# Token lists compacted by a one-hot product and stored as 16 runs, and queries scaled ahead, in a retention + experts + bilinear kernel

## The chip, the cores and the metric

One core of a Trainium2 chip runs the whole kernel. Its engines work from queues of their own: TensorE (PE) multiplies matrices into PSUM banks, VectorE (DVE) and ScalarE (ACT) do elementwise work, GpSimd (POOL) does elementwise work and issues indirect DMAs, and SyncE (SP) issues most of the other DMAs. The metric is device microseconds of one launch, the median of three runs.

## The reference

Three parts follow each other. `q`, `k`, `v` are 4 x 8 x 768 x 64.

```
# retention, per batch and head; gamma[h] = 1 - 2**(-5-h)
state = gamma*state + outer(k[t], v[t]);  y[t] = (q[t] @ state)/sqrt(64)
# x: 3072 tokens x 512. Top-1 of 8 experts, 512 -> 1024 -> 512
logits = x @ w_gate + bias[modality];  e = argmax(logits)
g = 1/(sum(exp(logits - max)) + 1e-9)
out[mask_e] = g * (relu(x[mask_e] @ w1[e]) @ w2[e])
# bilinear layer on the 3072 rows
y = ((x @ m1) * (x @ m2)) @ w3 @ w_out
```

## The kernel before

**Attention.** The 3072 tokens are 24 tiles of 128, six for each batch. A tile's decay is split: `vprime` multiplies the values by gamma^-(position) on POOL, and the result of a tile is multiplied by a table `gtab[t % 6]` that holds gamma^(position)/8. The loop over `t` from -1 to 24 issues, in a fixed order that no scheduler changes, work of several tiles: `scores(t+1)` (k transposed by q, masked on VectorE into `at`), `rows_gate(t-1)`, `attend_T(t)` (state by q), `attend_v(t)` (masked scores by v', then `xT` on VectorE with the table), and `state(t+1)`. `rows_gate` multiplies `xT` by the identity and the gate's columns at once: ScalarE copies the rows `xr` out and issues their store to `x_scratch`, VectorE sums the logits into `L`. The transposed keys `kT` of every tile are loaded beside `qkv`.

**Fold.** w3 @ w_out is computed on the chip. The weights come as float64 bits: `f64_f32` decodes a piece in three VectorE passes, ScalarE casts the high part, and the low part is a subtraction (POOL in the loop, VectorE after it). Seven of the twelve pieces are decoded between the tiles; `fold_mm(n)` then issues n of 64 units of three products, the counts being the list `FM`.

**Token lists.** Tiles are routed in batches of 8, 7, 6 and 3. `route_a` finds the expert of each token as a one-hot row `OH`, and running counts `RS`; `route_b` turns them into the place of each token in its expert's list. `scatter_ids(t)` stores 128 pairs (token, gate), 8 bytes each, to their places in `tok_scratch`, one indirect DMA a tile; the 24 are declared free of each other. After the loop `tables1` computes which list piece each slot takes and gathers the pieces (`lists`), `tables2a` and `tables2b` make the control rows `ctl`, `tables3` the gather indices, and the expert slots begin, whose products fill TensorE up to the end. `cld` keeps the lists in slot order, and is read back near the end for the final scatter.

Order around the change: the loop body and the calls behind it, as the program's text has them; each engine takes its instructions in that order. Rotating PSUM banks (`bank()`, five) and tile pools of fixed depth (`QB` for qkv, three `xr`) make later instructions wait for earlier readers.

Of the kernel before, what the change touches and what calls it, by code (L numbers as in the profile page):

```python
# [18 lines left out]
P = 128  # L19
B, H, S, D = 4, 8, 768, 64  # L20
NT = B * S
E = 8
# [13 lines left out]
LOAD_T = [2, 5, 8, 10, 13, 15, 18, 20, 22]  # L36
SPLIT_T = [5, 8, 10, 13, 15, 18, 20]
QB, KB, FB = 7, 5, 5
# [14 lines left out]
for _n, _w in (("ident", 128), ("sl", 128), ("ones", 128), ("desc", 8), ("er", 8), ("kp", NPAIR), ("le", 64), ("gt", 64), ("p", 1), ("tok", NTILE)):  # L53
    CB[_n] = (_o, _o + _w)
    _o += _w
# [3 lines left out]
def const_tables():  # L59
# [27 lines left out]
    put(b, CB, "er", (e * R)[None, :])  # L87
# [4 lines left out]
    put(b, CB, "p", i[:, None])  # L92
    return a.astype(np.float32), b.astype(np.float32)


def pack(q, k, v, moe_modality_id, moe_w_gate, moe_modality_bias, moe_w1, moe_w2, moe2_w1, moe2_w2, moe2_w3, moe2_w_out):
# [7 lines left out]
    kT = qt(k)  # L104
# [7 lines left out]
    def bits(a):  # L112
# [9 lines left out]
        "mod": moe_modality_id.reshape(NTILE, P).T,  # L122
        "mbias": moe_modality_bias.reshape(1, 16),
        "wg": kmaj(moe_w_gate, 4),
    }
FM = [6, 12, 8, 8, 8, 6]


def kernel(tc, a, out):
# [3 lines left out]
    with ExitStack() as ctx:  # L133
# [39 lines left out]
        RS = ct([P, NTILE + 1, E], F32, "RS")  # L173
# [3 lines left out]
        dsti = ct([P, NTILE], I32, "dsti")  # L177
        tg = ct([P, NTILE, 2], F32, "tg")
        cg = ct([P, NTILE, 2], F32, "cg")
# [3 lines left out]
        lists = fold.tile([P, T2, 2], F32, name="lists")  # L183
# [11 lines left out]
        def f64_f32(pool, tag, s, nm, done, bufs=2):  # L195
            d = pool.tile([P, 1024], U32, tag=tag, name="dec" + nm, bufs=bufs)
            V.tensor_scalar(d, s[:, :, 1], 3, 0x3FFFFFFF, op0=ALU.logical_shift_left, op1=ALU.bitwise_and)
            yield
            V.scalar_tensor_tensor(d, s[:, :, 1], 0xC0000000, d, op0=ALU.bitwise_and, op1=ALU.bitwise_or)
            yield  # L200
            V.scalar_tensor_tensor(d, s[:, :, 0], 29, d, op0=ALU.logical_shift_right, op1=ALU.bitwise_or)
            yield from done(d.bitcast(F32))
# [84 lines left out]
        none = lists[:TR + 1]  # L287
        st = {}

        def load(t):  # L290
            s = st.setdefault(t, {})
            s["kT"] = pa.tile([P, 4, P], F32, tag="kT", name=f"kT{t}", bufs=KB)
            nc.sync.dma_start(s["kT"].rearrange("p a i -> p (a i)"), a["kT"][t])
# [32 lines left out]
        def attend_v(t):  # L326
# [7 lines left out]
            V.tensor_tensor(s["xT"], b, gtab[t % NC], op=ALU.mult)  # L334
# [18 lines left out]
        def rows_gate(t):  # L353
            s = st[t]
            xr = pa.tile([P, 4, P], F32, tag="xr", name=f"xr{t}", bufs=3)
# [7 lines left out]
            nc.scalar.dma_start(xd[t * P:t * P + P, :], xr.rearrange("p a w -> p (a w)"))  # L363
# [3 lines left out]
        def route_a(t0, t1):  # L367
            sl, sh = slice(t0, t1), [P, t1 - t0, E]
            V.tensor_tensor(L[:, sl], L[:, sl], biasm[:, sl], op=ALU.add)
            V.tensor_reduce(mx[:, sl, 0], L[:, sl], axis=AX.X, op=ALU.max)  # L370
            V.tensor_tensor(tmp[0][:, sl], L[:, sl], bc(mx[:, sl], sh), op=ALU.is_equal)
            V.tensor_tensor(tmp[0][:, sl], tmp[0][:, sl], bc(CV("desc").unsqueeze(1), sh), op=ALU.mult)
            V.tensor_reduce(dst[:, sl, 0], tmp[0][:, sl], axis=AX.X, op=ALU.max)
            V.tensor_tensor(OH[:, sl], tmp[0][:, sl], bc(dst[:, sl], sh), op=ALU.is_equal)
            for t in range(t0, t1):
                V.tensor_tensor(RS[:, t + 1, :], RS[:, t, :], OH[:, t, :], op=ALU.add)
            V.tensor_tensor(tmp[1][:, sl], L[:, sl], bc(mx[:, sl], sh), op=ALU.subtract)
            nc.scalar.activation(tmp[1][:, sl], tmp[1][:, sl], AF.Exp)

        def route_b(t0, t1):  # L380
            sl, sh, w = slice(t0, t1), [P, t1 - t0, E], (t1 - t0) * E
            b = bank()
            nc.tensor.matmul(b[:, :w], lhsT=CV("sl"), rhs=OH[:, sl].rearrange("p t e -> p (t e)"), start=True, stop=False)
            nc.tensor.matmul(b[:, :w], lhsT=CV("ones"), rhs=RS[:, sl].rearrange("p t e -> p (t e)"), start=False, stop=True)
            V.tensor_reduce(dst[:, sl, 0], tmp[1][:, sl], axis=AX.X, op=ALU.add)
            V.tensor_scalar(dst[:, sl, 0], dst[:, sl, 0], 1e-9, None, op0=ALU.add)
            V.reciprocal(tg[:, sl, 1], dst[:, sl, 0])
            V.tensor_tensor(tmp[0][:, sl], b[:, :w].rearrange("p (t e) -> p t e", e=E), bc(CV("er").unsqueeze(1), sh), op=ALU.add)
            V.tensor_tensor(tmp[0][:, sl], tmp[0][:, sl], OH[:, sl], op=ALU.mult)
            V.tensor_reduce(dst[:, sl, 0], tmp[0][:, sl], axis=AX.X, op=ALU.add)  # L390
            V.tensor_copy(dsti[:, sl], dst[:, sl, 0])
# [5 lines left out]
        def scatter_ids(t):  # L397
            nc.gpsimd.memset(pad, 0.0)
# [816 lines left out]
```

## Time and profile before

| | us |
|---|---|
| median of 3 runs (884.88 to 885.59) | 885.41 |
| the profiled execution | 886.3 |
| its span | 884.2 |
| TensorE busy / VectorE / ScalarE / GpSimd | 839.0 / 478.6 / 286.8 / 342.0 |

The span runs from the first to the last recorded instruction. Busy time of TensorE is modelled at its ends; a gap between two of its instructions is a wait. "Releaser" is what ended the idle time ahead of an instruction, inferred from semaphores. DMA share is the mean busy share of the 16 DMA engines.

### The profile page before, as it was taken

Reading aid. Unit: us, or ns where it says so; the run is one execution under the profiler, and the core shown is the slowest. Engines: PE = TensorE matmul, PEld = TensorE weight load, DVE = VectorE, ACT = ScalarE, POOL = GpSimd, SP = SyncE. Lnnn points to the kernel's source line nnn. Section 1 sums busy time; section 2 is a strip of 40 time slices with the busy share of each in tenths; the row PEclk is TensorE's granted clock in tenths of the full one; section 3 lists DMA queues with packets and bytes.
Section 4 is the critical chain, followed back from the end, with each engine's and each line's share of the span. In section 5 each row is a group of like instructions: output and inputs, shape, how many; then the busy total and the mean of one; then the engine's idle time right before and its main releaser. Section 6 shows DMA issues by size and latency. Waiting matters only on the chain. (4 is left out here: it accounts for less than half of the span.)

```text
span 884.2 us, 16215 instructions
## 1 busy us (share of the span) xinstructions
PE 839.0 (95%) x6240; PEld 767.5 (87%) x6240; DVE 478.6 (54%) x697; ACT 286.8 (32%) x514; POOL 342.0 (39%) x324
## 2 busy tenths in 40 slices
PE   5988788899999999999999999999999999999997
PEld 5988687689999999899999977887887888999996
DVE  4476586764432516751111653255237375999993
ACT  1232232143213222722211533142223343455541
POOL 4238184223005041814100314246326354666563
PEclk9999899999999999999999999999999999999999
DMA  8999984778236445754326029714111514744411
GB/s 304 323 409 235 322 210 99 204 271 310 89 121 215 144 160 198 268 190 154 111 61 252 26 62 408 277 55 155 60 58 50 156 48 143 236 159 155 144 51 58
DMA packets 63187, 153.67 MB, mean 174 GB/s; under 512 B 10675, under 2 KB 22963, under 8 KB 61544
## 3 DMA queue, kind: packets, MB, share of 16 engines
q1 hardware_dynamic: 51736, 122.64, 41.1%
q0 software_dynamic: 7888, 23.36, 7.7%
q10 hardware_dynamic: 3456, 6.29, 2.3%
q8 instruction: 60, 0.98, 0.5%
q14 instruction: 47, 0.39, 0.1%
HBM read 102.73 MB, written 49.58 MB: 172 GB/s over the span
## 5 line engine op out<-in xcount | busy, mean ns | idle before, releaser
L235 PE MATMUL b<-h,wh 128*128 128x256 f32 x768 | 139.8, 284 | 1.4 <-PE b L645 0.7
L851 PE MATMUL al<-xh,ws 128*128 128x512 f32 x384 | 125.1, 394 | 2.0 <-DMA ws<-ws_scratch 1.4
L235 PEld LDWEIGHTS b<-h,wh 128*128 128x128 f32 x768 | 119.8, 192 | 2.2 <-ACT h L760 0.9
L761 DVE SCALAR_TENSOR_TENSOR h<-b,h 128x512 fp32r<-128x512 f32 x48 | 32.6, 688 | 158.1 <-ACT h L760 155.9
L235 PE MATMUL b<-xh,wl 128*128 128x256 f32 x384 | 108.8, 283 | 0.3 <-DVE wl L206 0.3
L235 PE MATMUL b<-xh,wh 128*128 128x256 f32 x384 | 108.8, 283 | 0.1
L235 PE MATMUL b<-h,wl 128*128 128x256 f32 x384 | 108.7, 283 | 0.1
L235 PE MATMUL b<-xl,wh 128*128 128x256 f32 x384 | 108.7, 283 | 0.0
L851 PEld LDWEIGHTS al<-xh,ws 128*128 128x128 f32 x384 | 72.2, 188 | 19.3 <-issue 1.8
L851 PE MATMUL al<-xl,ws 128*128 128x512 f32 x192 | 75.6, 394 | 0.0
L1135 PE MATMUL oa<-wfh,ab 128*128 128x256 f32 x384 | 74.9, 284 | 0.7 <-DVE ot L1142 0.6
L235 PEld LDWEIGHTS b<-xh,wl 128*128 128x128 f32 x384 | 73.7, 192 | 0.5 <-DVE wl L206 0.5
L235 PEld LDWEIGHTS b<-xh,wh 128*128 128x128 f32 x384 | 73.6, 192 | 0.4 <-issue 0.3
L235 PEld LDWEIGHTS b<-xl,wh 128*128 128x128 f32 x384 | 73.6, 192 | 0.0
L235 PEld LDWEIGHTS b<-h,wl 128*128 128x128 f32 x384 | 73.7, 192 | 0.0
L851 PE MATMUL ga<-xh,ws 128*128 128x512 f32 x192 | 63.7, 392 | 2.3 <-ACT p L964 1.7
L1135 PEld LDWEIGHTS oa<-wfh,ab 128*128 128x128 f32 x384 | 61.6, 189 | 2.6 <-DVE ot L1142 2.0
L760 ACT ACTIVATE h<-b 128x512 fp32r<-128x512 f32 x48 | 28.4, 596 | 86.4 <-PE b L235 84.8
L206 POOL TENSOR_TENSOR wo<-dec,wo 128x512 fp32r<-128x512 f32 x12 | 16.6, 1393 | 99.5 <-ACT wo L205 99.5
L1135 PE MATMUL oa<-wfl,ab 128*128 128x256 f32 x192 | 54.0, 281 | 0.0
L796 ACT COPY yT<-b 128x512 f32<-128x512 f32 x24 | 14.1, 588 | 118.7 <-PE b L235 106.0
L636 POOL DMA_INDIRECT xg<-x_scratch,gidx x28 | 28.0, 1001 | 63.1 <-PE b L645 44.2
(224 smaller groups left out, 1887.2 us busy)
## 6 DMA issues: line engine op xcount, KB each, us to landing
qkv<-in_qkv SPq DMA_DIRECT2D x22, 768.0 KB
ws_scratch<-wo SPq DMA_DIRECT2D x28, 512.0 KB
ws<-ws_scratch SPq DMA_DIRECT2D x28, 512.0 KB
raw<-in_wall SPq DMA_DIRECT2D x24, 512.0 KB
ab<-ab_scratch SPq DMA_DIRECT2D x24, 512.0 KB
f64f<-in_w SPq DMA_DIRECT2D x8, 1024.0 KB
f64m<-in_m SPq DMA_DIRECT2D x16, 512.0 KB
y_scratch<-yT SPq DMA_DIRECT2D x14, 512.0 KB
```

Of the source, the lines that this page charges most:

```text
L206: lo_eng.tensor_tensor(lo, src, hi.bitcast(F32), op=ALU.subtract)
L235: nc.tensor.matmul(b, lhsT=x, rhs=y, start=first and n == 0, stop=last and n == 3 * len(ks) - 1)
L636: nc.gpsimd.indirect_dma_start(out=xgs[j][y], out_offset=None, in_=xd, in_offset=bass.IndirectOffsetOnAxis(ap=gidx[:, y, j:j + 1], axis=0))
L760: nc.scalar.activation(h, b, AF.Relu)
L761: V.scalar_tensor_tensor(l, b, 0.0, h.bitcast(F32), op0=ALU.max, op1=ALU.subtract)
L796: nc.scalar.copy(yT[:, 2 * dp:2 * dp + 2, :].rearrange("p a t -> p (a t)"), b)
L851: nc.tensor.matmul(b, lhsT=y, rhs=r[:, kk, :], start=first and n == 0, stop=n == 5, skip_group_check=True)
L1135: nc.tensor.matmul(b, lhsT=x[:, k], rhs=y[:, k], start=first and n == 0, stop=n == 11, skip_group_check=True)
```

## The change

1. **Lists.** The rank of a token is now counted inside a group of 1, 2 or 3 tiles (`GROUPS`). `places` compares the ranks with a row of numbers, which gives a one-hot matrix 128 x w for each tile; `entries` multiplies `OHV` (expert one-hot times token number, and times gate: 16 columns) by it, so that 16 rows, two for each expert, hold that group's entries in order and densely. They are copied to `ls` and stored with one indirect DMA as 16 runs of w numbers, each at its offset `gix`; a later run writes over the unused end of an earlier one, so the stores are in turn. Token and gate lists lie apart, in two halves of `tok_scratch`, and `tables1` gathers twice.
2. **Queries.** `decayed` multiplies q in place by the table ahead of the scores, on VectorE, two or three tiles early; `xT` becomes a ScalarE copy.
3. **Work dealt out.** Route operations, one-hot rows and decoding are generators with a cost each; `spend` takes up to 2.4 us of them a tile.
4. **Others.** Keys 0 to 3 are transposed on TensorE instead of loaded; constants are loaded in parts; the x stores go from ScalarE's queue to SP's; the low part of the weights goes to VectorE; six buffers for qkv, four for kT, two for xr; `FM` changes; the lists are read back as 24 rows and transposed.

```diff
-LOAD_T = [2, 5, 8, 10, 13, 15, 18, 20, 22]
-SPLIT_T = [5, 8, 10, 13, 15, 18, 20]
-QB, KB, FB = 7, 5, 5
+LOAD_T = [0, 1]
+SPLIT_T = [2, 4, 6, 8, 10, 13, 16]
+BUDGET = 2.4
+QB, KB, FB = 6, 4, 5
+GROUPS = [(1,) * 8, (2, 2, 3), (3, 3), (3,)]
-FM = [6, 12, 8, 8, 8, 6]
+FM = [3, 22, 12, 8, 8, 6]
...
+        def decayed(t, eng=V):
+            q = st[t]["qT"]
+            eng.tensor_tensor(q, q, gtab[t % NC], op=ALU.mult)
...
-            V.tensor_tensor(s["xT"], b, gtab[t % NC], op=ALU.mult)
+            if t:
+                nc.scalar.copy(s["xT"], b)
+            else:
+                V.tensor_tensor(s["xT"], b, gtab[0], op=ALU.mult)
...
-            nc.scalar.dma_start(xd[t * P:t * P + P, :], xr.rearrange("p a w -> p (a w)"))
+            nc.sync.dma_start(xd[t * P:t * P + P, :], xr.rearrange("p a w -> p (a w)"))
...
+        def places(g0, g1):
+            w, ohs = (g1 - g0) * P, []
+            for t in range(g0, g1):
+                oh = pa.tile([P, 3 * P], F32, tag="oh", name=f"oh{t}", bufs=3)[:, :w]
+                V.tensor_scalar(oh, io[:, :w], rk[:, t], None, op0=ALU.is_equal)
+                ohs.append(oh)
+            return ohs
+
+        def entries(x, g0, g1, ohs):
+            w = (g1 - g0) * P
+            b = bank()[:2 * E, :w]
+            for i, oh in enumerate(ohs):
+                nc.tensor.matmul(b, lhsT=OHV[:, g0 + i].rearrange("p z e -> p (z e)"), rhs=oh, start=i == 0, stop=i == g1 - g0 - 1)
+            ls = pa.tile([2 * E, 3 * P], F32, tag="ls", name=f"ls{g0}", bufs=1)[:, :w]
+            nc.scalar.copy(ls, b)
+            nc.gpsimd.indirect_dma_start(out=tbl.rearrange("r i -> (r i)").rearrange("(r w) -> r w", w=w), out_offset=bass.IndirectOffsetOnAxis(ap=gix[:, x:x + 1], axis=1), in_=ls, in_offset=None)
...
-        def scatter_ids(t):
-            nc.gpsimd.memset(pad, 0.0)
-            i = nc.gpsimd.indirect_dma_start(out=tblf, out_offset=bass.IndirectOffsetOnAxis(ap=dsti[:, t:t + 1], axis=0), in_=tg[:, t, :], in_offset=None)
-            no_dep(i.ins, "ids", "each scatter writes entries of its own")
...
+        def decoded(x):
+            g = fold_split(x, V)
+            yield from timed(g, (.7, 1.2, 1.2))
+            late.append(g)
+            more.append(x + 2)
...
+            if t >= 1:
+                spend(BUDGET)
...
         t0, t1 = bounds[-2], bounds[-1]
-        route_a(t0, t1)
+        run(routed(t0, t1))
+        for r in ready:
+            route_exp(*r)
         fold_mm(FM[0])
-        route_b(t0, t1)
-        for t in range(t0, t1):
-            scatter_ids(t)
+        b = route_mm(t0, t1)
+        ready.clear()
+        run(settled(t0, t1, b))
+        routes_done()
         tables1()
```

VectorE in the middle of the loop, about one turn and a half, before (`at` is the mask, `L` the gate reduce, `decf` a decoded piece):

```order
L315 TENSOR_TENSOR at_1022<-b_1023,ca_sb 128x4x128
L315 TENSOR_TENSOR at_1022<-b_1024,ca_sb 128x4x128
L362 TENSOR_REDUCE L<-r_1037 128x8
L334 TENSOR_TENSOR xT_1059<-b_1046,g_97 128x512
L315 TENSOR_TENSOR at_1077<-b_1078,ca_sb 128x4x128
L315 TENSOR_TENSOR at_1077<-b_1079,ca_sb 128x4x128
L197 TENSOR_SCALAR decf_1092<-f64f_1012 128x1024
L362 TENSOR_REDUCE L<-r_1095 128x8
L334 TENSOR_TENSOR xT_1117<-b_1104,g_98 128x512
L199 SCALAR_TENSOR_TENSOR decf_1092<-f64f_1012,decf_1092 128x1024
```

The same place after the change (`oh` is a one-hot row block, `wol` the low part of a weight piece):

```order
L343 TENSOR_TENSOR at_950<-b_951,ca_sb 128x4x128
L343 TENSOR_TENSOR at_950<-b_952,ca_sb 128x4x128
L393 TENSOR_REDUCE L<-r_964 128x8
L322 TENSOR_TENSOR qkv_817<-qkv_817,g_97 128x512
L467 TENSOR_SCALAR oh_1000<-io_sb,rk 128x128
L226 TENSOR_TENSOR wol_93<-decf_815,woh_89 128x1024
L201 TENSOR_SCALAR decf_1005<-f64f_686 128x1024
L203 SCALAR_TENSOR_TENSOR decf_1005<-f64f_686,decf_1005 128x1024
L343 TENSOR_TENSOR at_1014<-b_1015,ca_sb 128x4x128
L343 TENSOR_TENSOR at_1014<-b_1016,ca_sb 128x4x128
```

The xT multiply out of a bank is gone; a multiply of qkv in SBUF, the one-hot rows and the low part have come in between the gate reduce and the next mask.

ScalarE in the loop, two turns before (`xr` are the rows, `T` the state):

```order
L361 COPY xr_1036<-r_1037 128x256 x2
L363 DMA x_scratch<-xr_1036 128x512
L351 COPY T_102<-acc_886 64x4x64 x2
L361 COPY xr_1094<-r_1095 128x256 x2
L363 DMA x_scratch<-xr_1094 128x512
L351 COPY T_101<-acc_886 64x4x64 x2
```

And after (`ls` is the list of one group):

```order
L392 COPY xr_1027<-r_1028 128x256 x2
L477 COPY ls_1039<-b_1037 16x128
L363 COPY xT_1055<-b_1042 128x512
L382 COPY T_100<-acc_926 64x4x64 x2
L224 CAST w3h_1003<-decf_1005 128x1024
L392 COPY xr_1093<-r_1094 128x256 x2
L477 COPY ls_1105<-b_1103 16x128
L363 COPY xT_1121<-b_1108 128x512
L382 COPY T_101<-acc_926 64x4x64 x2
```

The list copy and the xT copy stand between the rows and the state copies, and the store of the rows is no longer in this queue.

TensorE behind the loop, around the last batch's rank products, before (the fold's products are those of `woh`, `wol`):

```order
L246 MATMUL b_1611<-wol_93,w3h_1090 128x512
L246 MATMUL b_1611<-woh_89,w3l_1091 128x512
L383 MATMUL b_1630<-OH,cb_sb 128x24
L384 MATMUL b_1630<-RS,cb_sb 128x24
L417 MATMUL b_1646<-RS,cb_sb 128x8
L246 MATMUL b_1611<-woh_90,w3h_1090 128x512
L246 MATMUL b_1611<-wol_94,w3h_1090 128x512
```

And after:

```order
L251 MATMUL b_1758<-wol_91,w3h_1003 128x512
L251 MATMUL b_1758<-woh_87,w3l_1004 128x512
L435 MATMUL b_1768<-OH,cb_sb 128x24
L437 MATMUL b_1768<-rel,cb_sb 128x24
L439 MATMUL b_1768<-cb_sb,RS 16x1
L475 MATMUL b_1786<-oh_1780,OHV 16x384
L475 MATMUL b_1786<-oh_1782,OHV 16x384
L475 MATMUL b_1786<-oh_1784,OHV 16x384
L498 MATMUL b_1793<-RS,cb_sb 128x8
L251 MATMUL b_1758<-woh_87,w3h_1003 128x512
```

The three list products of the last group stand between its rank products and the totals (L417, now L498), and so ahead of most of the fold; six more of them stand ahead of the first fold product.

## Rows read from the trace of the kernel before

**Rows 1.** Windows: busy us and instructions by engine, granted clock, DMA share, GB/s

```profile
0.00:26.09 26.09, 16.19 (x168) 15.05 (x168) 9.95 (x17) 3.58 (x8) 10.52 (x17) 0.87 0.86 298
26.09:145.10 119.01, 103.56 (x1304) 94.53 (x1300) 81.33 (x170) 35.38 (x90) 56.89 (x61) 0.96 0.93 285
145.10:199.40 54.30, 49.02 (x231) 40.46 (x230) 37.15 (x78) 14.28 (x21) 15.88 (x22) 0.97 0.64 202
199.40:884.20 684.80, 670.20 (x4546) 617.51 (x4544) 350.17 (x433) 233.60 (x395) 258.75 (x225) 1.00 0.42 148
28.00:64.00 36.00, 34.62 (x474) 31.86 (x472) 23.22 (x48) 10.22 (x28) 9.61 (x8) 1.00 0.98 375
72.00:96.00 24.00, 19.15 (x256) 17.35 (x254) 14.28 (x22) 6.77 (x16) 15.70 (x19) 0.95 1.06 202
```

**Rows 2.** Timeline of TensorE, one tile: start, us, engine, line, operation, tiles

```profile
30.69 1.16 PE L313 MATMUL b<-qkv,kT 64*128 64x128 f32 x16
31.78 1.19 PE L359 MATMUL r<-iwg,xT 128*128 128x136 f32 x8
32.81 1.05 PE L324 MATMUL b<-qkv,T 128*128 128x128 f32 x8
33.80 1.09 PE L332 MATMUL b<-at,vp 128*64 128x128 f32 x16
34.72 0.63 PE L348 MATMUL acc<-vp,qkv 128*64 128x64 f32 x16
35.29 0.94 PE L313 MATMUL b<-qkv,kT 64*128 64x128 f32 x12
```

**Rows 3.** The token list's DMAs: ns min/median/max, first and last start; landing

```profile
L399 POOL DMA_INDIRECT tok_scratch<-tg,dsti x24: 954/999/1829, 69.0 to 155.9; - x24
...
DMA to landing us min/median/max: 5.4/11.8/12.7
```

**Rows 4.** Timeline of POOL, the first v' product

```profile
9.21 1.04 POOL L304 TENSOR_TENSOR vp<-qkv,ca_sb 128x512 f32<-128x512 f32 x1 [7.37 <-DMA qkv<-in_qkv]
```

**Rows 5.** Timeline, 15 to 19 us: POOL's decay tables beside VectorE's bias work

```profile
15.11 3.15 POOL L506 TENSOR_TENSOR g<-ca_sb 128x512 f32<-128x512 f32 x3
...
15.22 1.15 DVE L539 TENSOR_TENSOR biasm<-mf,mb_sb 128x192 f32<-128x192 f32 x1
...
18.51 0.36 DVE L542 TENSOR_TENSOR biasm<-biasm,tmp 128x192 f32<-128x192 f32 x1
```

**Rows 6.** Timeline of VectorE in that tile; then one group of its lines

```profile
30.40 0.69 DVE L334 TENSOR_TENSOR xT<-b,g 128x512 f32<-128x512 f32 x1 [1.11 <-PE b L332]
...
31.89 1.29 DVE L315 TENSOR_TENSOR at<-b,ca_sb 128x512 f32<-128x512 f32 x2 [0.79 <-PE b L313]
...
33.69 0.19 DVE L362 TENSOR_REDUCE L<-r 128x8 f32<-128x32 f32 x1 [0.52 <-ACT xr L361]
...
L201 DVE SCALAR_TENSOR_TENSOR decf<-f64f,decf 128x1024 uint32<-128x1024 uint32 x7 | 8.6, 1223 | 0.2
```

**Rows 7.** Landing of plain stores and loads of another scratch tensor

```profile
DMA to landing us min/median/max: 2.6/3.5/5.0
```

**Rows 8.** Timeline of TensorE: control rows, and one unit of the fold

```profile
164.54 0.45 PE L457 MATMUL b<-cb_sb,c 128*1 128x32 f32 x10 [4.01 <-DVE c L452]
...
198.24 0.39 PE L246 MATMUL b<-woh,w3l 128*128 128x512 f32 x1
...
198.92 0.40 PE L246 MATMUL b<-woh,w3l 128*128 128x512 f32 x1
```

**Rows 9.** Timeline of VectorE: from the control copy to the last split

```profile
165.03 0.31 DVE L458 CAST ctl<-b 1x160 int32<-1x160 f32 x1 [0.64 <-PE b L457]
...
178.99 0.69 DVE L197 TENSOR_SCALAR decf<-f64f 128x1024 uint32<-128x1024 uint32 x1 [2.52 <-issue]
...
192.63 1.23 DVE L221 TENSOR_TENSOR w3l<-decf,w3h 128x1024 fp32r<-128x1024 f32 x1 [1.17 <-ACT w3h L219]
```

More of the change, by code (lines that the diff above doesn't have):

```diff
@@ L1 @@
 import itertools
+from collections import deque
 from contextlib import ExitStack
@@ L182 @@
         pad = ct([1, 1], F32, "pad")
-        lists = fold.tile([P, T2, 2], F32, name="lists")
+        lists = fold.tile([P, 2, T2], F32, name="lists")
         woh = [fold.tile([P, 1024], F32R, name=f"woh{i}") for i in range(4)]
@@ L286 @@
         tmp.append(pa.tile([P, NTILE, E], F32, name="tmp2"))
-        none = lists[:TR + 1]
+        none = lists[:TRP]
+        io = pa.tile([P, 3 * P], F32, name="io_sb")
+        OHV = pa.tile([P, NTILE, 2, E], F32, name="OHV")
+        rk = pa.tile([P, NTILE, 1], F32, name="rk")
+        gate = pa.tile([P, NTILE, 1], F32, name="gate")
+        rel = pa.tile([P, 8, E], F32, name="rel")
         st = {}
@@ new lines, in timed, with routed, settled @@
+        def timed(g, costs):
+            for c in costs:
+                if next(g, g) is g:
+                    return
+                yield c
+        bounds = list(np.cumsum([0] + BATCHES))
+        pend, ready, late, more, listed, rq, dq = [], [], [], [], [], deque(), deque()
+        small = itertools.repeat(.24)
+        def routed(t0, t1):
+            yield from timed(itertools.chain(route_a(t0, t1), route_rel(t0, t1)), small)
+            ready.append((t0, t1))
+        def settled(t0, t1, b):
+            yield from timed(route_b(t0, t1, b), small)
+            pend.extend((t0 + x, *g) for x, g in enumerate(groups(t0)))
@@ new lines, in decoded, with finish, spend @@
+        def decoded(x):
[3 more added lines that the diff above has]
+            more.append(x + 2)
+        def finish():
+            for g in late:
+                next(g)
+                dq.appendleft(timed(g, (1.2,)))
+            late.clear()
+        def spend(us):
+            while us > 0:
+                q = rq or (dq if not late else None)
+                if not q:
+                    return
+                c = next(q[0], None)
+                if c is None:
+                    q.popleft()
+                else:
+                    us -= c
@@ L525 @@
-            if t in SPLIT_T:
-                work = fold_split(SPLIT_T.index(t))
-            next(work, None)
-            if t - 1 >= 0:
+                keys(1)
+                decays(1, V)
+                decayed(1, V)
+                warm(4)
+            if 1 <= t and t + 1 < NTILE:
+                scores(t + 1)
+            if 1 <= t and t + 2 < NTILE:
+                keys(t + 2)
+            if t >= 2:
                 rows_gate(t - 1)
+            settle()
             if 0 <= t < NTILE:
```

259 lines of the change are left out of this document (177 added, 82 removed).

## Prediction

> **What bounds the kernel now.** I read the windows first, because the change touches two stretches only. [rows 1] cuts the span of 884.2 us at 26.09 (the scores of tile 3 start), at 145.10 (the values of tile 23 are multiplied) and at 199.40 (the first expert slot begins). In the last 684.8 us TensorE is busy for 670.2 us: it is the bound there, the change leaves its products alone, and I carry 684.8 over. So the question is 199.4 us: the start, the attention loop, and the stretch between loop and slots that folds w3 with w_out while the token lists are settled.
>
> Next I read one undisturbed tile on TensorE [rows 2]: scores at 30.69, rows and gate 31.78, state product 32.81, values 33.80, state update 34.72, next scores 35.29. That is 1.09 + 1.03 + 0.99 + 0.92 + 0.57 = 4.60 us with no gap, so TensorE sets the pace when nothing disturbs. From tile 3's scores to tile 23's values there are 21 scores, 22 rows, 19 state products (none at tiles 6, 12, 18), 22 values and 17 updates: 22.9 + 22.7 + 18.8 + 20.2 + 9.7 = 94.3 us. The stretch takes 119.0. Some 25 us are lost.
>
> Where they go shows in the scatters of list entries [rows 3]: 24 of them, about 1.0 us each on POOL, but their landing takes 5.4 to 12.7 us, median 11.8. In the 24 us from 72 the DMA engines are as full as from 28 to 64 (share 1.06 against 0.98), yet move 202 GB/s instead of 375 [rows 1]: the 8-byte entries hold engines and carry nothing. In these 24 us TensorE is busy for 19.2. The transfers of x and of queries queue among them.
>
> **The start.** The first v' product waits for its data until 9.21 [rows 4]. Ahead of and with that data SP queues 1890 KB (two kT, two q, the constants, k and v of tile 0); now 930 KB (identity, q and k, the small constants, v), as keys 0 to 3 are transposed on TensorE. 960 KB at the 298 GB/s of the first window is 3.2 us. The bias work on VectorE, 3.7 us from 15.22 to 18.87 ahead of the first xT [rows 5], moves into the loop. Against that stand 16 transposes before tile 3's scores, at a quarter of 1.03 us each 4.1 us, if no wait hides them; TensorE is busy for 16.2 of the 26.1 us, so some of them will be hidden. So 2.8 to 6.9 us are won; I take 5.1: the scores of tile 3 at 21.0.
>
> **The loop, TensorE.** The lists now cost products: 8 of 128 columns, 4 of 256, and 3 of 384 before tile 23. By the 136-column rows product (1.03 / 4 = 0.26) they take 0.24, 0.49 and 0.73 each: 6.1 us, and the rank and offset products some 2 more. TensorE's floor becomes 94.3 + 8.1 = 102.4.
>
> **The loop, VectorE.** The mask stays, 1.29 a tile, and the gate reduce, 0.19 [rows 6]. The xT multiply of 0.69 goes to ScalarE as a copy; in its place the query is scaled ahead. No row has that operation, both inputs in SBUF with 512 columns; bounds are 0.36 for 192 columns [rows 5] and 1.22 for a pass of 1024 [rows 6]; I take half of the latter, 0.61. The low half of each decoded weight comes over from POOL, 1.22, so a decode is 0.69 + 3 x 1.22 = 4.35 [rows 6, 9]. Until tile 23's mask: 21 x 1.29 + 20 x 0.19 + 20 x 0.61 + 7 x 4.35 = 73.5, about 58 route operations at 0.24 = 14, and the one-hot rows 3: 90.5 us. The plan deals it out at 2.4 us a tile.
>
> What this leaves out is the port. POOL's three products of 1.05 us stand beside a VectorE multiply of 192 columns that takes 1.15 us, where a like one alone takes 0.36 [rows 5]: it stood still until POOL had finished. The mask and xT (one input in PSUM) keep 1.29 and 0.69 [rows 6]. The v' product of POOL now meets operations that can be held, 20 times. Held in full, VectorE needs 90.5 + 20 x 1.04 = 111; not at all, 90.5. Half is 101, level with TensorE. Two engines in fixed orders that are equally full don't overlap perfectly, and tile 14 stores two lists in one turn; I add 5.6 and take 108.0 for the stretch, 11 less than now.
>
> **The loop, ScalarE and SP.** ScalarE takes on xT (about 0.6 us, as xT's 0.69) and the list copies, and loses the issue of the x stores. Behind the list copy stand xT and the state copies: one buffer holds the list, so the copy waits until the last store landed. Nearest rows for that landing: 2.6 to 5.0, median 3.5, for plain stores [rows 7]; 5.4 at least for the old scatter. With 3.5 a turn takes 0.4 + 1.0 + 3.5 + 0.2 = 5.1 us, 0.5 over a tile, which the slack of about 2.7 us before the rows product covers over four turns; that is in the 5.6. The x stores go to SP's queue, between loads five tiles ahead; from 28 to 64 such loads were fed at 4.6 us a tile, so I cost this move at nothing; without that cover it is rival 3.
>
> **From the loop to the slots.** Now 54.3 us. Here the change adds, on the path: 9 list products of 384 columns, 6.6 us; and TensorE waits before two groups of them for VectorE's gate reduce and three one-hot rows (1.5) and for the eight route operations and three rows (2.5): 4.0. It removes the 4.01 us for which the control rows are waited for [rows 8], since 22 units of the fold, not 12, now stand ahead of them. That is paid back later. A unit is 0.68 us (198.24 to 198.92). Behind the control rows 39 units are left, not 46. VectorE's work there is unchanged: from the control copy at 165.03 to the end of the last weight split at 192.63 + 1.23 = 193.86 is 28.8 us [rows 9], 26.3 without the 2.52 in which it waited for a load delayed by the scatters. Unit 56 needs that split, and TensorE is there after 31 units, 21.1 us: it waits 5.2. The sum is 54.3 + 6.6 + 4.0 - 4.0 + 5.2 = 66.1, with the clock loss of now (0.97 granted). If the split comes in time and the clock stays up it is about 58. I take 63.0, nearer the first, since the chain stands in rows.
>
> The end (the list read back as 24 rows and transposed) is a fraction of a microsecond; nothing waited for its old form. Sum: 21.0 + 108.0 + 63.0 + 684.8 = 876.8. The profiled execution took 886.3, 2.1 over its span, and lies 0.9 over the median of 885.41: 876.8 + 2.1 - 0.9 = 878.0.
>
> **Rivals.** 1. *TensorE's pace.* The port costs little because POOL's v' falls beside the mask, and the DVE chain of the fold is not late: 19.2 + 102.4 + 58 + 684.8 + 1.2 = 866. For it: the tiles from 28 to 64 run at the floor. Against it: VectorE was half empty then.
>
> 2. *The port (slower).* Every v' holds VectorE in full, 111, and the same 5.6 of poor overlap: 117; the fold keeps all its waits, 66: 21 + 117 + 66 + 684.8 + 1.2 = 890. It decides from about 0.8 us held a tile, where the loop reaches 112. For it: [rows 5]; against it: a late VectorE would be at the mask, which isn't held, when v' starts. The Trainium skill (SBUF — State Buffer, Who interferes with whom) states this as an exclusive lock, taken also by a VectorE operation with two SBUF inputs when the GpSimd one reads SBUF, so that the second to issue blocks fully. The 1.15 against 0.36 agrees, and the page speaks against scaling queries in SBUF instead of xT out of PSUM.
>
> 3. *The list stores (slower).* If a store of 16 runs lands no sooner than the quickest old scatter, 5.4 us, a turn is 7.0: four turns from tile 9 lose 3 x 2.4, the six stores from tile 14 take 35 where four tiles take 18.4; less the slack, about 18 us: 102.4 + 18 = 120, and 65 behind it: 892. It begins to cost at a landing of 3.5 us and turns the balance at about 4.5. The Trainium skill (DMA: Bandwidth & Descriptors, Anatomy of one DMA) gives some 2 us fixed for such a small transfer; by that a turn would be 3.6 and nothing would wait. No row here is that short.
>
> 4. *Won and given back.* The scatters cost less than they seem and the full DMA engines pace the loop at 115, with 63 behind: 885.
>
> **Chances.** 878 gets 0.45 (its own range 872 to 883), rival 1 0.25, rival 2 0.13, rival 3 0.10, rival 4 0.07. Faster by over 0.2% (what a measurement here can tell): 0.70; within: 0.07; slower: 0.23. The range of 864 to 891 takes in the forecast, rival 1, rival 4 and most of rival 2.
>
> **What would show it.** The DMA engines at 350 GB/s or more until the loads end; tile 3's scores near 21; tile 23's values near 129; a gap on TensorE at the control rows gone, and one of some 5 us ahead of the last fold products. VectorE rows of 2 us beside v' speak for rival 2; ScalarE waiting for the list scratch, for rival 3. I am wrong if the stretch before tile 23's values takes over 119 us, or if the last 684.8 us move.

## The result: 1.3% slower

The changed kernel takes 895.66 us (median of 4 executions, 894.23 to 898.45), the kernel before 885.14 us on the same chip: ratio 1.0126, 95% interval 1.0095 to 1.0157. The forecast was 878, range 864 to 891. The profiled execution took 898.45 us, 2.8 over the median, with a span of 896.7.

The windows of the changed kernel, cut at the same places as [rows 1] (scores of tile 3, end of the values of tile 23, first product of slot 0), and two stretches of the loop:

```profile
0.00:19.97 19.97, 16.51 (x193) 15.08 (x193) 9.96 (x16) 6.80 (x14) 8.81 (x15) 1.00 0.91 326
19.97:144.65 124.68, 110.64 (x1358) 96.72 (x1354) 96.98 (x201) 48.39 (x123) 37.01 (x33) 0.96 0.74 277
144.65:213.50 68.85, 60.37 (x247) 42.09 (x247) 39.87 (x89) 16.27 (x25) 12.17 (x11) 0.93 0.45 158
213.50:896.70 683.20, 670.25 (x4548) 617.32 (x4546) 349.73 (x434) 233.91 (x395) 259.03 (x225) 1.00 0.41 148
28.00:64.00 36.00, 32.42 (x425) 29.93 (x424) 30.56 (x54) 15.54 (x36) 9.06 (x7) 0.95 0.98 371
72.00:96.00 24.00, 20.68 (x276) 17.88 (x272) 20.99 (x40) 9.75 (x27) 7.88 (x7) 1.00 0.88 327
```

| stretch (us) | before | forecast | changed |
|---|---|---|---|
| start, to tile 3's scores | 26.09 | 21.0 | 19.97 |
| loop, to the end of tile 23's values | 119.01 | 108.0 | 124.68 |
| loop to slot 0 | 54.30 | 63.0 | 68.85 |
| the rest | 684.80 | 684.8 | 683.20 |

The start won 6.1 us and the DMA jam of 72 to 96 us is gone (327 GB/s, before 202). But the loop grew by 5.7 us and the stretch behind it by 14.6. TensorE's waits in the loop (waiter, releaser, us in total, times, longest):

```profile
PE r L390 <- ACT xT L363: 7.4, 4, 4.2
PE b L341 <- DMA kT<-in_kT: 6.3, 4, 2.0
```

ScalarE copies xT behind the list copy, and that copy waits for the store before it (ScalarE's waits in the loop; then the DMAs of the token table, in place of [rows 3]):

```profile
ACT ls L477 <- DMA tok_scratch<-ls,gix: 18.6, 5, 7.4
```

```profile
L478 POOL DMA_INDIRECT tok_scratch<-ls,gix x14: 844/871/1491, 76.2 to 162.8; - x14
...
DMA to landing us min/median/max: 2.0/3.3/7.1
```

The worst case, on all engines: the store of 103.08 us and a 1 MB weight load are issued together, the next list copy starts only at 110.24, and TensorE gets no xT until 111.16, by when it runs at a lowered clock (0.66 granted from 110 to 120 us, the rows product 2.18 us for 1.19).

```profile
102.55 0.25 ACT L477 COPY ls<-b 16x128 f32<-16x128 f32 x1
...
103.08 0.87 POOL L478 DMA_INDIRECT tok_scratch<-ls,gix  x1 [2.17 <-ACT ls L477]
103.11 0.38 SPq L196 DMA_DIRECT2D f64f<-in_w  x1
...
110.24 0.26 ACT L477 COPY ls<-b 16x128 f32<-16x128 f32 x1 [7.43 <-DMA tok_scratch<-ls,gix]
...
110.55 0.56 ACT L363 COPY xT<-b 128x512 f32<-128x512 f32 x1
...
111.16 2.18 PE L390 MATMUL r<-iwg,xT 128*128 128x136 f32 x8 [4.20 <-ACT xT L363]
```

SP's queue up to the end of the loop. A weight load (L196) waits until VectorE has decoded the weight two before it, an x store (L394) until ScalarE has copied the rows; the loads of queries and keys stand behind both:

```profile
SPq L394 <- ACT xr L392: 59.3, 19, 8.7
SPq L196 <- DVE decf L205: 18.9, 6, 4.4
```

Behind the loop, VectorE meets TensorE at the totals, the control rows and the list transposes (start, us; in brackets the wait), in place of [rows 8, 9]:

```profile
162.31 0.17 DVE L499 COPY rt_n<-b 128x8 f32<-128x8 f32 x1 [3.63 <-PE b L498]
...
177.76 0.31 DVE L540 CAST ctl<-b 1x160 int32<-1x160 f32 x1 [3.99 <-PE b L539]
...
187.10 0.20 DVE L547 CAST gidx<-b 128x38 int32<-128x38 f32 x1 [0.32 <-PE b L545]
...
191.06 0.69 DVE L201 TENSOR_SCALAR decf<-f64f 128x1024 uint32<-128x1024 uint32 x1 [1.93 <-DMA f64f<-in_w]
...
204.58 1.23 DVE L226 TENSOR_TENSOR w3l<-decf,w3h 128x1024 fp32r<-128x1024 f32 x1 [1.11 <-ACT w3h L224]
```

The same three steps before the change:

```profile
153.00 0.16 DVE L418 COPY rt_n<-b 128x8 f32<-128x8 f32 x1
165.03 0.31 DVE L458 CAST ctl<-b 1x160 int32<-1x160 f32 x1 [0.64 <-PE b L457]
```

From the loop's end: totals after 17.7 us (before 7.9), control rows 15.5 later (12.0), slot 0 another 35.7 later (34.1). So 9.8 + 3.5 + 1.6 us were lost, in that order. (Slot 0's first product before the change stands at 199.16, two products ahead of the 199.40 of [rows 1]; this sum is therefore 0.3 us over the table's.) VectorE is busy for 39.9 of the 68.9 us.

### The profile page after: what moved, and what is told of

It reads as the page before. It is cut to its first block, busy times and chain, and to the rows that moved or that the text cites. A ratio compares the mean times of both kernels' runs of the same rounds, so it can differ in the third digit from the quotient of the medians.

```text
span 896.7 us, 16513 instructions
## 1 busy us (share of the span) xinstructions
PE 857.8 (96%) x6339; PEld 771.2 (86%) x6339; DVE 496.5 (55%) x739; ACT 305.4 (34%) x556; POOL 317.0 (35%) x283
## 3 DMA queue, kind: packets, MB, share of 16 engines
q8 instruction: 62, 1.02, 0.5%
## 5 line engine op out<-in xcount | busy, mean ns | idle before, releaser
L240 PEld LDWEIGHTS b<-xh,wl 128*128 128x128 f32 x384 | 73.6, 192 | 0.5 <-DVE wl L211 0.5
L240 PEld LDWEIGHTS b<-xh,wh 128*128 128x128 f32 x384 | 73.6, 192 | 0.4 <-issue 0.3
L240 PEld LDWEIGHTS b<-xl,wh 128*128 128x128 f32 x384 | 73.6, 192 | 0.0
L240 PEld LDWEIGHTS b<-h,wl 128*128 128x128 f32 x384 | 73.6, 192 | 0.0
L980 ACT COPY yT<-b 128x512 f32<-128x512 f32 x24 | 14.1, 588 | 118.6 <-PE b L240 118.6
L1323 PE MATMUL oa<-wfl,ab 128*128 128x256 f32 x192 | 53.8, 280 | 0.0
```

Source lines behind the costliest of these rows:

```text
L240: nc.tensor.matmul(b, lhsT=x, rhs=y, start=first and n == 0, stop=last and n == 3 * len(ks) - 1)
L980: nc.scalar.copy(yT[:, 2 * dp:2 * dp + 2, :].rearrange("p a t -> p (a t)"), b)
L1323: nc.tensor.matmul(b, lhsT=x[:, k], rhs=y[:, k], start=first and n == 0, stop=n == 11, skip_group_check=True)
```

## The experiments

Ratios are against the kernel before on the same chip. Loop and "behind" are the two middle stretches of one profiled execution each; four profiles of programs with the same loop (changed, e4, e6, e9) gave 121.3 to 124.7, so less than 3 us there proves nothing by itself. "Tile 10" is the start of its scores (before the change 57.9). The first one-hot row of the lists comes at 71.8 us in the changed kernel, so up to tile 10 changed, e1, e4, e5, e6, e9 and e11 are one and the same program, and so are e7, e10, e12 and e14: tile 10 came at 55.9 to 59.5 in the first seven, at 53.3 to 57.4 in the other four. The stretch from slot 0 on takes 683 to 687 us in these profiles (e9: 688.6), so a gain ahead of it need not reach the total in full.

| run | ratio (95%) | tile 10 | loop | behind |
|---|---|---|---|---|
| changed | 1.0126 (1.0095-1.0157) | 57.8 | 124.7 | 68.9 |
| e1_ls2 | 1.0054 (1.0028-1.0080) | 56.8 | 118.6 | 67.3 |
| e2_xact | 1.0191 (1.0156-1.0225) | 63.2 | 129.4 | 69.0 |
| e3_late | 1.0108 (1.0063-1.0153) | 59.5 | 125.5 | 65.6 |
| e4_tail | 1.0159 (1.0125-1.0192) | 58.1 | 121.3 | 74.3 |
| e5_nolist | 0.9856 (0.9832-0.9881) | 59.5 | 112.7 | 55.9 |
| e6_ctl | 1.0141 (1.0124-1.0158) | 57.9 | 124.7 | 65.2 |
| e7_kfirst | 1.0076 (1.0060-1.0093) | 57.4 | 123.9 | 65.8 |
| e9_fm4 | 1.0240 (1.0214-1.0266) | 58.0 | 122.8 | 71.7 |
| e10_three | 1.0018 (0.9994-1.0042) | 54.8 | 116.2 | 65.6 |
| e11_nostore | 0.9998 (0.9975-1.0021) | 55.9 | 115.4 | 69.2 |
| e12_single | 1.0085 (1.0058-1.0112) | 53.3 | 114.0 | 74.0 |
| e13_half | 1.0042 (1.0011-1.0074) | 55.7 | 117.4 | 65.2 |
| e14_tail2 | 0.9930 (0.9913-0.9946) | 54.1 | 115.9 | 58.3 |
| e15_early | 0.9940 (0.9925-0.9955) | 53.8 | 115.7 | 58.3 |
| e16_both | 1.0122 (1.0101-1.0144) | 56.8 | 122.8 | 66.4 |
| e17_wq | 0.9914 (0.9885-0.9943) | 53.1 | 110.5 | 58.7 |
| e18_wq0 | 1.0081 (1.0054-1.0108) | 53.2 | 116.7 | 65.6 |

### What the list work costs: e5, e11, e1, e12

e5: no one-hot rows, products, copies or stores. e11: the stores alone left out.

> The changed kernel without the list entries: no one-hot rows, no list products, no list copies and stores; the ranks, tables and everything else stay. Every list then holds token 0, and the output rows are scattered by row number. It prices all the list work. If the lists are what lost the gain (theory L: the list's 13 us of products, the waits of ScalarE for the stores and what these delay), loop to tile 23's values falls from 124.7 to 106 to 112 us, the stretch behind it from 68.9 to 52 to 56, the total to 868 to 876. If the DMA engines pace the loop anyway (theory D), the scores of tile 10 stay at 57 to 58 us and the loop stays above 115: total 880 or more.

> The changed kernel without the 14 stores of list runs alone; one-hot rows, list products and their copies stay (every list then holds token 0, and output rows are scattered by row number). With no list work at all it took 1.4% less than before, 2.7% less than the changed kernel. Theory S (the landing of the stores and the single scratch): most of that comes back, 876 to 880, and the loop takes 115 to 117 us instead of 124.7. Theory W (the products on TensorE, the one-hot rows on VectorE and the chain that they stretch): at most 8 us come back, 887 to 891; behind the loop the stretch stays at 65 or more, since no engine waits long for a store there.

All list work costs 2.7% (1.0126 to 0.9856), some 24 us: 12.0 in the loop, 13.0 behind it in the profiles. Without the stores alone 1.3% come back, some 11 us, 9.3 of them in the loop and none behind it. So in the loop it is mostly the stores (theory S), behind it the rest (theory W); neither was right for both. The total, 0.9998 (885 us by the ratio), lies between the two forecasts. Some of these differences arise ahead of tile 10, where the programs are the same: counted from tile 10's scores to the end of the loop, all list work costs 13.0 us (86.8 to 73.8), the stores 7.9, and the single scratch (e1, next) 4.6.

e1, a second scratch, used in turn with the first:

```diff
+            if turn[0] % 2:
+                ls = lists[:2 * E].rearrange("p z t -> p (z t)")[:, :w]
+            else:
-            ls = pa.tile(..., tag="ls", name=f"ls{g0}", bufs=1)[:, :w]
+                ls = pa.tile(..., tag="ls", name=f"ls{g0}", bufs=1)[:, :w]
+            turn[0] += 1
```

> The changed kernel with two list scratches in turn instead of one (895.7 us). Theory L (the single list scratch is what lost the loop): ScalarE's 18.6 us of waiting for list stores in the loop fall below 6, the 4.2 us wait of the rows product for xT at 111 goes, the loop stretch (tile 3's scores to tile 23's values, 124.7 us) falls to 114 to 118, the total to 886 to 890. Theory P (the wait only moves): GpSimd then waits for the store before, stands in front of its v' products, and the total stays within 893 to 897. Theory D (the DMA engines' load by tile 10 lost the lead): the first ten tiles are as slow as before, tile 10's scores still near 57.8 us, whatever happens later.

```profile
ACT lists L483 <- DMA tok_scratch<-lists,gix: 2.0, 1, 2.0
```

Theory L: ScalarE's waits for list stores in the loop fall from 18.6 to 2.0 us, TensorE's for xT from 7.4 to 1.5, the loop by 6.1, the ratio by 0.7%. The total missed its range by 2.5 us, the loop by 0.6. Theory D was right about tile 10 (56.8), but no list store stands ahead of tile 10, so this could not have come out otherwise.

e12, on top of e10: `GROUPS = [(1,) * 8, (1,) * 7, (1,) * 6, (3,)]`.

> The run with three edits, with lists stored tile by tile except the last three (22 groups instead of 14): a list product then has 128 columns, not 256 or 384, 0.24 instead of 0.49 or 0.73 us. 18 products of 0.6 us less come to 8 to 9 us of TensorE, 4 of them behind the loop; against that 8 stores more, about 1 us each on GpSimd and 2 to 3.3 us to land. Theory W (work on TensorE and VectorE is what the lists cost): 5 to 8 us less than the run with three edits, 1% faster. Theory S (the stores are what they cost): ScalarE waits for the scratches again, 3 us less at best, or slower.

A miss for theory W; "or slower" of theory S came. The loop gained 2 us at most, the stretch behind it lost 8.4: more and smaller lists were left for it, ScalarE waits 13.6 us there for the two scratches, and VectorE 14.5 us for the last batch's offset product, which stands behind them on TensorE. Smaller products don't pay if each brings a store.

### The loop's first ten tiles: e2, e3, e7, e13, e16, e15, e18

e2: `nc.scalar.dma_start(xd[...], ...)`. e3: `LOAD_T = [2, 5]`, `SPLIT_T = [5, 8, 10, 13, 15, 17, 19]`, `BUDGET = 3.4`. e7: `load_k(t + 3)` moved ahead of `load(x)`.

> The changed kernel with the x stores back on ScalarE's queue. Theory Q (a load of keys stands in SP's queue behind an x store that waits for the rows): the four waits of the scores for kT (6.3 us) go, tile 10's scores come at 53 instead of 57.8 us, total 890 to 893. Theory D (the DMA engines are full until about 75 us: share 0.98 from 28 to 64): the loads land no earlier, the waits for kT stay at 5 us or more, and ScalarE pays 0.33 us of issue per tile: 895 to 898.

> The changed kernel with the fold weights loaded and decoded at the turns of the kernel before (loads from turn 2, decodes at turns 5, 8, 10, 13, 15, 17, 19; up to 3.4 us of VectorE work a turn instead of 2.4, so that all seven still fit). Theory D: without three of the six 1 MB loads ahead of tile 10 (some 2.8 us each at 371 GB/s) the waits for kT go, and tile 10's scores come at 52 to 54 us instead of 57.8. Theory Q: tile 10's scores stay within 1.5 us of 57.8. The total depends on whether the decodes then collide with the lists: 889 to 893 if they do not, 895 to 899 if they do.

> The changed kernel with the load of a tile's keys (needed two tiles later) ahead of the load of queries, keys and values five tiles later in SP's queue; two lines exchanged. Theory K (a matter of order: the urgent 256 KB stand behind 768 KB that have time, and at times behind a 1 MB weight load): the four waits for kT (6.3 us) fall below 2, tile 10's scores come at 52 to 54 instead of 57.8 us, total 4 to 5 us lower. Theory D (a matter of throughput: 22.8 MB have to pass by then, at 371 GB/s some 61 us): the wait moves to the queries and values, tile 10's scores stay at 56 to 58, total within 2 us.

e2 fell out slower than either theory said: the waits for kT became 10.7 us, tile 4's scores alone waited 4.2. Theory Q's gain did not come, but e2 is no clean test of the x store: with it out of the way SP stood elsewhere, 7.5 us at a load of queries that waited for an x store to land, and 53.0 us (18.9 in the changed kernel) for decodes. e18 below clears the x stores. e3: tiles 3 to 8 followed each other at 3.7 to 4.6 us (tile 8's scores at 42.7, changed 45.0), then tile 9's waited 4.1 us for kT; tile 10 (59.5) came later than either theory said, and the total did not move. e7: the waits for kT fell to 0.3 us, but tile 9's scores still came at 51.2 (changed 51.6), and tile 10 as D said. The total gained 0.5%, about what theory K said and more than D allowed. The profiled execution took 894.87 us, the other three 892.0 to 892.2, and the same order of loads gave tile 10 at 53.3 to 54.8 in e10, e12 and e14: so tile 10 in e7's profile does not speak for D.

e13 and e16: half of each weight's load, without and with e3's turns.

> The changed kernel with half of every fold weight's load (0.5 MB instead of 1; the decode reads the half twice, so that VectorE's work is the same, and the folded weights are not the reference's). Theory D (until tile 10 the DMA engines' throughput paces the loop, 22.8 MB at some 371 GB/s): 2.6 to 3.1 MB less are 7 to 8 us, tile 10's scores come at 51 to 53 us instead of 57 to 59 as in every kernel so far but one, the waits for kT go below 1 us, the total falls by 4 to 7 us. Theory K (single late loads, not throughput): tile 10's scores stay at 56 or later.

> The changed kernel with both: half of every fold weight's load, and the decodes at the turns of the kernel before. Late decodes alone ran at TensorE's pace to tile 8 (42.7 us) and then lost 5 us to loads that came together; half loads alone ran no faster to tile 8 (45.5) but came to tile 10 2.1 us earlier (55.7). Theory VD (VectorE's decodes hold tiles 4 to 8, the loads tiles 9 and 10, each by itself): both together bring tile 10's scores to 51 to 53 us. If one resource alone were behind both, 55 to 58.

e13 fell between its theories: no faster to tile 8 (45.5), and at tile 10 (55.7) level with the earliest of the seven programs above (55.9). Its total is clear of the changed kernel's, 0.8% or some 7 us less, with waits for kT of 1.0 us: here theory D was right, and the bytes have a price in the total. Here a second resource shows: tile 5's scores waited for the scaled query, which VectorE ran beside v' in 1.40 us, elsewhere 0.68:

```profile
29.96 1.04 POOL L320 TENSOR_TENSOR vp<-qkv,ca_sb 128x512 f32<-128x512 f32 x1 [2.11 <-PE b L362]
...
30.15 1.40 DVE L324 TENSOR_TENSOR qkv<-qkv,g 128x512 f32<-128x512 f32 x1
...
31.60 0.60 PE L343 MATMUL b<-qkv,kT 64*128 64x128 f32 x6 [1.33 <-DVE qkv L324]
```

e16 speaks against theory VD: with half the bytes and late decodes tile 9's scores came at 50.5 again, 8.1 us after tile 8's, and tile 10's at 56.8. At these turns neither fewer bytes nor VectorE's load moved them, and the total (1.0122) is that of e3 and of the changed kernel. SP's queue in e16 shows what stood ahead of them (start, us):

```profile
37.12 0.33 SPq L396 DMA_DIRECT2D x_scratch<-xr  x1
37.49 4.67 SPq L196 DMA_DIRECT2D f64f<-in_wout  x2
42.27 1.33 SPq L308 DMA_DIRECT2D qkv<-in_qkv  x1
43.64 0.43 SPq L315 DMA_DIRECT2D kT<-in_kT  x1
```

From 37.5 to 42.2 SP stood at a weight load whose buffer VectorE was still decoding (until 41.8), and the loads of tiles 9 and later waited behind it. The Trainium skill (DMA: Bandwidth & Descriptors, Anatomy of one DMA) says that the DMA engines wait for no semaphore, a wait happens on the issuing sequencer ahead of the dispatch; the trace agrees, 18.9 us of it in the changed kernel.

e18 takes the weight loads from the third on out of SP's queue and issues them from ScalarE's, e17 does so on top of e14:

```diff
-            for g in late:
+            for g, x in late:
                 next(g)                  # ScalarE's copy, which waits for the same decode
+                queue[0] = nc.scalar
+                fold_load(x)
+                queue[0] = nc.sync
...
-            while more:
-                fold_load(more.pop(0))
```

> The changed kernel with that edit alone. Theory Q2: tile 10's scores come at 53 to 55 instead of 57.8 us, SP's waits for decodes (18.9 us) go, total from 1.3% to 0.6 to 0.9% over before. Theory D: tile 10's scores stay at 57 or later, total unchanged within 0.3%.

> The fastest version so far (three edits and the new order behind the loop, 0.7% under before) with the loads of the fold weights, from the third on, issued from ScalarE's queue, right behind the copy that waits for the same decode. In SP's queue such a load waits for VectorE to have decoded the weight two before it (in the changed kernel six times, 18.9 us in all), and the loads of queries and keys stand behind it. Theory Q2 (SP's order holds tiles 8 to 10): tile 10's scores come at 50 to 52.5 instead of 54.1 us, total 2 to 4 us lower, 0.9 to 1.2% under before. Theory D (throughput): tile 10's scores stay at 53.5 or later and the total moves by less than 1.5 us.

Tile 10's scores and the window from 20 to 46 us in the changed kernel, then the same in e18, and e18's waits of TensorE for kT and of SP for the rows:

```profile
57.84 1.16 PE L341 MATMUL b<-qkv,kT 64*128 64x128 f32 x16
...
20.00:46.00 26.00, 22.80 (x314) 20.98 (x312) 22.40 (x32) 11.68 (x28) 10.14 (x8) 1.00 0.97 374
...
53.17 1.16 PE L343 MATMUL b<-qkv,kT 64*128 64x128 f32 x16
...
20.00:46.00 26.00, 23.98 (x322) 22.07 (x322) 21.53 (x31) 11.54 (x28) 9.98 (x8) 1.00 1.02 403
...
PE b L343 <- DMA kT<-in_kT: 0.8, 1, 0.8
...
SPq L396 <- ACT xr L394: 73.6, 21, 6.4
```

In both, tile 10's scores come at 53.1 to 53.2 us, the waits for kT are 0.8 us or less, and the engines move 403 and 409 GB/s from 20 to 46 us where they moved 374. SP's waits for decodes are gone from the loop (e14 had 27.3 us of them), while the x stores are still in its queue and it waits 73.6 us for their rows; tiles 8 to 10 follow each other at 4.6 and 4.8 us all the same, so these stores do no harm there. For e18 theory Q2 holds: 53.2 us lies 2.7 us ahead of the earliest of the seven programs above. For e17 it is not shown: 53.1 us lies between the ranges of both theories and beside e12's 53.3, and the total falls by 1.4 us (0.9930 to 0.9914), no more than D allowed; its loop is 5.4 us shorter than e14's in the profiles. By their totals e18 and the changed kernel, and e17 and e14, are not told apart (the intervals overlap). e15, the queries of tiles 4 and 5 scaled a turn earlier:

> The run before this one, with the queries of tiles 4 and 5 scaled a turn earlier (and their decay tables too). Theory V (in the first ten tiles VectorE, busy 22.4 of 26 us, is late with the scaled queries that the scores need one turn later: in the run with half loads the scores of tile 5 waited 1.33 us for them): tile 6's scores come 1 to 2 us earlier, and tile 10's 0 to 2. Theory D (the loads hold tiles 5 to 10): no change within 0.5 us at tile 10. The total moves by less than 0.2% by either.

Tile 6's scores came 1.3 us earlier (33.7 against 35.0), tile 10's 0.3, the total did not move: theory V's wait is real, and small.

### Behind the loop: e4, e9, e6, e10, e14

e4: one decode ahead of the last gate reduce, tables ahead of the last list. e9: the same with `FM = [3, 6, 28, 8, 8, 6]`. e6: the changed kernel with `FM = [3, 15, 19, 8, 8, 6]`.

> The changed kernel with one weight decode (x = 7) moved ahead of the last tile's gate reduce and list rows on VectorE, and the control tables' arithmetic ahead of the last batch's list; nothing is added or left out. Theory V (behind the loop VectorE's chain of tables and five decodes sets the first slot; it began at 162.3 us, 9.3 later than before the change): the next decode begins 6 to 8 us earlier, TensorE's waits for w3h (3.5 us) go, loop to slots falls from 68.9 to 61 to 63, total 888 to 891. Theory T (TensorE's own products and its lowered clock set it: 60.6 of 69.1 us busy): only those 3.5 to 4.6 us go, loop to slots 64.5 to 66, total 891 to 893.

> The run with one decode and the control tables moved ahead, now with 6 units of the fold between the last list and the control rows instead of 22 (and 28 instead of 12 behind them). Theory C (slot 0 follows the control rows by 34 to 36 us): VectorE's wait for them (16.0 us there) falls to 3 to 5, the control rows come at about 169 us and slot 0 at 203 to 206 instead of 216.3; total 889 to 892, against 901.5. Theory T: slot 0 not earlier than 210, since TensorE has the same products to do.

> The changed kernel with 15 units of the fold between totals and control rows instead of 22, and 19 instead of 12 behind them; nothing else. Theory C (slot 0 follows the control rows by 34 to 36 us, through the five weight decodes and the expert's weight loads that stand behind them; before 165.0 to 199.2, changed 177.8 to 213.5, with one decode moved ahead 35.8): VectorE's wait of 4.0 us for the control rows goes, and slot 0 comes 3.5 to 4.5 us earlier, total 1% over the kernel before falls to 0.7 to 0.9%. Theory T (TensorE's own products set it): VectorE's chain gets shorter and TensorE waits for the control rows instead; no change within 1 us.

Two misses in a row. VectorE's own waits, e4 and then e9:

```profile
DVE ctl L543 <- PE b L542: 16.0, 1, 16.0
```

```profile
DVE gidx L550 <- PE b L548: 10.5, 1, 10.5
```

Work taken off VectorE's queue ahead of the control rows only made it wait there, since TensorE had 22 units to do first; with 6 units it waited at the list transposes instead, behind 28. e6 gained 3.6 us behind the loop in its profile, but nothing in its time (1.0141): not shown. e10 joins e1, e7 and e6:

> The changed kernel with three of the edits together: two list scratches in turn, the keys' load ahead of the queries', 15 units of the fold ahead of the control rows instead of 22. If the losses are separate (the wait for list stores, 6 us; the order of loads, 4 us; the control rows, 0 to 3.6 us), they add up: from 1.3% over the kernel before to within 0.2% of it, 884 to 888. If two of them only fill the same gap (the lead is lost to the DMA engines by tile 10 whatever else is done), 0.4 to 0.7% over.

They add up: level with before. e14 then reorders the stretch (in short form, calls by name; `FM = [8, 2, 2, 18, 8, 8, 6]`):

```diff
-        fold_mm(FM[0]); b = route_mm(t0, t1); settled; lists; tables1()
-        decode 7; tables2a(); fold_mm(FM[1]); tables2b()
+        b = route_mm(t0, t1); tables1(); fold_mm(8); tables2a(); tables2b()
+        settled; list (fold_mm(2)); list (fold_mm(2)); gathers; decode 7
```

> The run with three edits, with the stretch behind the loop in another order: the last batch's routing and the control tables stand ahead of the last two groups' lists on VectorE, 8 units of the fold ahead of the control rows, then the two lists between pairs of units, then the five weight decodes without a rendezvous between. The work is the same. Theory V (what the lists cost behind the loop, 12 of 24 us, is VectorE's chain, which lists and control rows hold up while VectorE is idle for 29 of 69 us): loop to slots falls from 65.6 to 56 to 60, the total to 0.4 to 0.9% below the kernel before. Theory T (TensorE's list products and its lowered clock): 63 or more, level with before within 0.2%.

```profile
142.99 0.17 DVE L505 COPY rt_n<-b 128x8 f32<-128x8 f32 x1 [0.94 <-PE b L504]
...
149.53 0.31 DVE L549 CAST ctl<-b 1x160 int32<-1x160 f32 x1 [0.55 <-PE b L548]
...
170.56 0.20 DVE L556 CAST gidx<-b 128x38 int32<-128x38 f32 x1 [1.79 <-PE b L554]
```

Theory V: the same work takes 58.3 us instead of 65.6. Totals come 6.8 us after the loop, control rows 6.5 later. Of the 7.3 us, 2.9 are a shorter busy time of TensorE (57.5 in e10, 54.7), at a granted clock of 1.00 for 0.95; that the clock rose because the waits went is likely and not tested. The kernel is 0.7% faster than before, and 0.9% faster than e10. e17 adds the loads and has the lowest ratio, 0.86% under before; its loop and the stretch behind:

```profile
20.58:131.10 110.52, 106.49 (x1358) 92.76 (x1354) 96.06 (x200) 48.50 (x123) 36.18 (x33) 1.00 0.84 310
131.10:189.78 58.68, 54.82 (x248) 40.71 (x248) 39.65 (x89) 16.17 (x25) 12.19 (x11) 1.00 0.50 186
```

## Why the prediction was wrong, step by step

By its own sign, over 119 us before tile 23's values, the prediction was wrong. The profile lies 19.9 us over its sum: 16.7 in the loop, 5.9 behind it, less 2.6 in the other two stretches. In time, three edits are each clear of the noise (their intervals do not overlap with that of the run they are compared with): the second scratch 0.7% (e1), the keys' loads first 0.5% (e7), the new order behind the loop 0.9% (e10 to e14). e14 has them all and takes 0.9930 of the time before, some 879 us where 878 was forecast.

*The start.* Right: 19.97 against 21.0. But the lead was no longer there at tile 10 in the changed kernel (57.8 against 57.9).

*The products' floors.* Nearly right. With most waits gone (e17) the loop takes 110.5 us at full clock, against 108.0, and TensorE is busy for 106.5 of them, against a floor of 102.4. In the changed kernel VectorE is busy for 97.0 us, between the 90.5 and the 111 of the port's bounds and near the 101 taken.

*"I cost this move at nothing" (SP's queue).* This step failed, though not for the x stores, which e18 clears at tile 10. I counted what is moved into SP's queue and not what its older entries now wait for: five weight loads are issued by 58 us instead of two, and from the third on each waits for a decode that VectorE now spreads over turns (six waits, 18.9 us; before, one of 8.7). Taken out of the queue the loads are worth 4.6 us at tile 10 (e18), and in the profiles' loops 5.4 us (e14 to e17) and 8.0 (e18); in time it is 1.4 and 4 us, neither clear of the noise. What shows in time is the order of the loads in that queue, 0.5% (e7). "From 28 to 64 such loads were fed at 4.6 us a tile" was a row of a queue with other entries.

*The list stores, "that is in the 5.6".* This step failed too. The landing of 3.5 us that I took is near the median (3.3), but single stores take up to 7.1 us, that one beside a 1 MB load; with half the bytes in the loads and the decodes at the same turns, ScalarE's waits for stores are 6.2 us (e16) for 18.6 (e3). One scratch turned the late landings into 18.6 us of waits and 6.1 us of loop (e1), the stores as a whole into 9.3 (e11). Rival 3 had the mechanism and the place, and got 0.10. Its condition (5.4 us or more for every store) did not come, and its price of 18 us in the loop is twice what the stores cost; that its total of 892 lies near the measured one is luck, since other losses, in SP's queue and behind the loop, stand where it had the stores.

*"I take 63.0".* My own sum was 66.1; 68.85 came. The sum followed TensorE and priced the lists at 6.6 us of products. They act through VectorE's order instead: they hold the totals up by 9.8 us, the 22 units hold up the control rows by 3.5, and the five decodes stand behind both. The 2.52 us that the sum left out as a load delayed by the scatters (its row in [rows 9] names no load) came again, 1.93 us at 191.06, with the scatters gone. The clock adds to it: 0.93 granted instead of 0.97 is, as an estimate, some 2.7 us of the 68.9. That the order is the cause is shown by e14, with the same products, but for what the clock's own part may be. My other case, about 58 if the split comes in time and the clock stays up, is what e14 took (58.3).

*The rest.* Right: 683.2 for 684.8.

*Still open:* why half the bytes gained 0.8% with the early decodes (e13) and nothing with the late ones (e16), though ScalarE's waits for stores fell there to a third; so bytes and order are not fully separated. And how much of the 0.96 granted in the loop is a cause of its own and how much follows from the waits (e17, with few waits, has 1.00).

## What to carry to other kernels

When a queue gets a new entry or a transfer a new turn, list for every entry what it waits for; one that waits for compute may belong on an engine that waits for the same result anyway (shown here at tile 10, not in the total). Where two engines meet several times, moving one meeting only moves the wait to the next: put what others hang on (control rows) first, and check every meeting behind. A wait that the working prices by a median should be priced by its worst landing where one buffer holds it.

## What the runs showed of the hardware

VectorE operations with their inputs in SBUF were held beside GpSimd's products: the scaled query (1.40 for 0.68 us, e13 above) and two decode steps beside v' and a decay table of the changed kernel (alone 0.69 and 1.23 us, [rows 6, 9]):

```profile
24.31 1.04 POOL L318 TENSOR_TENSOR vp<-qkv,ca_sb 128x512 f32<-128x512 f32 x1 [2.56 <-issue]
24.34 1.57 DVE L201 TENSOR_SCALAR decf<-f64f 128x1024 uint32<-128x1024 uint32 x1
25.31 1.49 POOL L589 TENSOR_TENSOR g<-ca_sb 128x512 f32<-128x512 f32 x1
25.94 1.94 DVE L203 SCALAR_TENSOR_TENSOR decf<-f64f,decf 128x1024 uint32<-128x1024 uint32 x1
```

The mask, with one input in PSUM, was not held beside a decay table (1.29 us in e2; without one, at 32.40 in the changed kernel, it is 1.29 too), as the prediction assumed:

```profile
21.10 1.04 POOL L589 TENSOR_TENSOR g<-ca_sb 128x512 f32<-128x512 f32 x1
21.54 1.29 DVE L343 TENSOR_TENSOR at<-b,ca_sb 128x512 f32<-128x512 f32 x2 [1.51 <-PE b L341]
```

A DMA share of 0.98 did not mean that the engines could move no more: from 28 to 64 us the changed kernel moved 371 GB/s at 0.98, and with the queue in another order e18 moved 396 and e17 399, both at 1.02.
